# The small product on the identity, split in two and moved to the couple's end

## The chip, the cores and the metric

The kernel runs on one core of a Trainium2 chip, as one program. The metric is the device time of one execution in microseconds (us). A kernel's time is the median of its runs. TensorE multiplies matrices, VectorE and ScalarE work on elements and empty TensorE's results, GpSimd takes some element-wise work, and SyncE issues most transfers. In the profile they are PE (and PEld for its weight loads), DVE, ACT, POOL and SP.

## The reference

Attention with normalised queries and keys, and then a feed-forward block with SiLU. All is float32: 8 batches, 12 heads, 448 positions, head size 64; 768 model columns, 2048 inner columns.

```python
def rmsnorm(x, g):
    rms = np.sqrt(np.mean(x * x, axis=-1, keepdims=True) + 1e-06)
    return x / rms * g
q_n, k_n = (rmsnorm(q, g_q), rmsnorm(k, g_k))
scores = scale * np.matmul(q_n, k_n.transpose(0, 1, 3, 2))
scores = scores - np.max(scores, axis=-1, keepdims=True)
attn = np.exp(scores)
attn = attn / (np.sum(attn, axis=-1, keepdims=True) + 1e-09)
out = np.matmul(attn, v).astype(np.float32)
...
h = x @ w_in
g = h * (1.0 / (1.0 + np.exp(-h)))
return (g @ w_out).astype(np.float32)
```

Between the two blocks the heads of a position are laid side by side: `x` has 3584 rows of 768 columns.

## The kernel before

Two branches are built, and the inputs at hand take `bounded`. It works on "couples": four heads of one batch, that is, two pairs of heads. There are 24 couples (`NC`), and `c` counts them. Six couples (`GROUP`) make two batches. The order of work on each engine is the order in which the program issues it; nothing is rearranged by a scheduler. Tiles with several buffers rotate, and semaphores are put in where a buffer or a value is passed on.

For each couple the program runs `visit(c)` and then `between(c)`.

`visit(c)` issues the scores of couple c, their exponentials, and the weighing of the values with them. It begins with `scores(c, 0, 0)` (L750). Each `scores` takes the next of the two buffers of the PSUM tile `sc`; a buffer is two banks of 128 partitions x 512. The four products of a `scores` are 64x64 tiles of TensorE, at the four places of its array, and run beside each other. Each row half of the array writes a bank of its own. The same holds for `weigh` (L787), which adds into the banks `av0` and `av1`. Between two steps of the weighing, `turn` has VectorE or ScalarE copy one column into a bank (L763), and the weighing behind it waits for that copy.

`between(c)` prepares couple c+1 and does a share of the feed-forward product of the two batches finished before. That product is cut, in the manner of Strassen and Winograd, into seven products for each pair of blocks (`Seven`, L961), with additions on VectorE (L910) and GpSimd (L982, L985). Each of the seven is three matrix products with 128x128 weights and 448 columns. They go into the PSUM tile `mm` (two buffers) or, in some turns, into `sc`. `fill(others, prompt)` deals them out: it takes steps from the running product until the share is done. After every third step it issues the next entry of `prompt`; what is left of `prompt` and `others` comes at the end. A product may be cut by the end of a `fill` and be continued in the next.

The softmax sums of a couple are four products with `ones` (L830, 32 output partitions each). For most couples from 10 on (`LAGGED`) these are issued at the end of `between`, into `mm`; for the others they are issued before the second `fill`. The reciprocals of the sums (L839) follow on VectorE.

The change concerns the normalisation of the queries of later couples. From couple `LATE` = 9 on, the queries lie in "quarters" of 32 partitions: the 64 numbers of a head's row are cut into two runs of 32, which lie on neighbouring quarters. ScalarE squares them (`square`), VectorE adds up each run of 32 (`sum_squares`, L705) into a tile of 128 partitions x 28, and the two partial sums of a row have to be added across partitions. `scale(c)` does that on TensorE, with the matrix `ident`. It is the identity at first. At couple 7, `pair_up` copies each 32x32 identity block to the neighbouring quarter, so that each of the two 64x64 blocks on the diagonal holds four 32x32 identities and the rest is zero. One product with `ident` (L716) then gives both quarters the full sum. VectorE takes it from an `sc` buffer and applies 1/64 and the small constant (L717), GpSimd raises it to the power -1/2 (L720), and, from couple 12 on, GpSimd multiplies the rows of the queries with it (L729). For couples 9 to 11 VectorE does this multiplication, during the next visit (`scale_rows` in `weights_in_visit`).

`scale(c + 2)` is called in `between(c)` for c from 7 to 21, fifteen times. It is the last entry of the `prompt` of the second `fill`: the entries are the first of the softmax reciprocals, then the squares, the transposition of the keys (`flip`), the remaining entries with `sum_squares`, and `scale`. After that `fill` come `finish()` and `sum_x` at the end of a group of six, the softmax sums of a lagged couple (`sum_up`), a small activation on ScalarE (L1669) that has the table for the exponentials loaded, and then the next `visit`.

Of the kernel before, what the change touches and what calls it, by code (L numbers as in the profile page):

```python
# [542 lines left out]
def bounded(  # L543
# [3 lines left out]
    P, D, R, J, S = z.P, z.D, z.R, z.J, z.S  # L547
# [9 lines left out]
    GROUP, LATE = z.NPAIR, z.LATE  # L557
# [49 lines left out]
    def q_of(c):  # L607
        return rows_q[c % 2 if c < GROUP + 2 else 0]
# [101 lines left out]
    def scale(c):  # L710

        if c >= NC:
            return
        f = norm.rms[c % 2][:, 0:n]
        t = ps.tile([P, 2, BANK], F32, name="sc", bufs=2)[:, 0, 0:n]
        nc.tensor.matmul(t, ident, f, start=True, stop=True)  # L716
        nc.vector.tensor_scalar(  # L717
            out=f, in0=t, scalar1=1.0 / D, scalar2=1e-6, op0=ALU.mult, op1=ALU.add
        )
        nc.gpsimd.tensor_tensor(out=f, in0=f, in1=minus_half.to_broadcast([P, n]), op=ALU.pow)  # L720
        if c > SOON:
            scale_rows(c, nc.gpsimd)

    def scale_rows(c, engine):

        f = norm.rms[c % 2][:, 0:n]
        rows = q_of(c)[:, 0 : z.NK].rearrange("p (n e) -> p n e", e=z.Q)
        factor = f.rearrange("p (n one) -> p n one", one=1).to_broadcast([P, n, z.Q])
        engine.tensor_tensor(out=rows, in0=rows, in1=factor, op=ALU.mult)  # L729
# [75 lines left out]
    def sum_up(c):  # L805

        n = D // 2  # L810
        early = c < GROUP
        if c < GROUP:
            t = bank(S)
        elif c in LAGGED:
            t = ps_mm.tile([P, BANK], F32, name="mm")[:, 0:S]
        else:
            t = ps.tile([P, 2, BANK], F32, name="sc", bufs=2)[:, 0, 0:S]
        terms = [(0, lambda: weights(c, 0))]
        if early:
            terms = [(0, lambda: weights(c, LEFT - 1))] + terms + [(1, None)]  # L820
        if c in FULL:
            terms.insert(0, (1, None))
        if c == GROUP - 1:
            terms.insert(1, (0, lambda: weights(c, 1)))
        for k, (which, w) in enumerate(terms):
            if early and k == len(terms) - 2:
                yield
            for h in range(2):
                for i in range(2):
                    nc.tensor.matmul(  # L830
                        t[ds(h * D + i * n, n), :],
                        ones[:, which + i if which else 0],
                        left_weights(c)[:, h] if which else w()[:, i, h],
                        start=(k == 0), stop=(k == len(terms) - 1),
                    )

        def invert(half):
            rows = ts(half, S // 2)
            nc.vector.reciprocal(out=factors(c)[0][:, rows], in_=t[:, rows])  # L839

        def spread():
            mine = [a.rearrange("(h i p) s -> i h p s", h=2, i=2) for a in factors(c)]
            queues = (nc.sync, nc.gpsimd if c == GROUP - 1 else nc.sync)
            if c >= EARLY:
                nc.vector.tensor_copy(factors(c)[1], factors(c)[0])
                for i in range(2):
                    for h in range(2):
                        queues[h].dma_start(mine[i][1 - i, h], mine[i][i, h])
                return
            for h in range(2):  # L850
                for i in range(2):
                    nc.sync.dma_start(mine[1][i, h], mine[0][1, h])
            for h in range(2):
                nc.sync.dma_start(mine[0][1, h], mine[0][0, h])

        yield [lambda: invert(0), lambda: (invert(1), spread())]
# [160 lines left out]
    summed = set()  # L1017
# [552 lines left out]
    def run_all(work):  # L1570
        for piece in work:
            piece()

    def between(c):

        def transposes_and_sums():
            if c in LAGGED:
                first = [lambda: divide(c - 1, None)] if c - 1 in LAGGED else [lambda: None]
                return first + [lambda: None, lambda: flip(c + 1, "k"), gain]
            summing = sum_up(c)  # L1580
            if c < GROUP - 1:
                transpose_k(c + 1)
            if c < GROUP:
                next(summing)
            if c == GROUP - 1:
                reciprocals = next(summing)
                divide(c - 1, None)
                sum_x([0, 1], 0)
                run_all(reciprocals)
                return  # L1590
            if GROUP <= c < LATE - 1:
                transpose_k(c + 1)
            reciprocals = next(summing)
            if LATE - 1 <= c < NC - 1:
                reciprocals += [lambda: flip(c + 1, "k"), gain]
            if GROUP // 2 < c < EARLY:
                divide(c - 1, None)
            return reciprocals

        if c == GROUP - 1:  # L1600
            for _ in range(2):
                room.w_in.open()
            for i, t in enumerate(scratch):
                size = z.R, 2 * J * D
                rows = q_of(c + 2)[0 : z.R, ts(i, size[1])]
                nc.scalar.activation(t[0 : size[0], 0 : size[1]], rows, AF.Square)
            transposes_and_sums()
        if c < LATE - 1:
            transpose_q(c + 1)
        elif c < NC - 1:  # L1610
            flip(c + 1, "q")
        if c < GROUP // 2:
            inverting.extend(transposes_and_sums())
        elif c == GROUP - 1:
            transpose_k(c + 1)
        if c >= GROUP and c % GROUP == 0:
            fetched = range(AHEAD) if c == GROUP else ()
            columns = products - 2 * HW * S * len(fetched)
            work = halves_in(last_two(c), range(HF), plain_in, dict(begun), fetched, c + GROUP < NC)
            begin(work, columns, 2 * GROUP)  # L1620
            begun.clear()
        late = add(c, LEFT - 1) if c >= GROUP else []
        if c >= GROUP and c not in FULL:
            late += add(c, LEFT)
        further = normalise(c + 2) if c >= GROUP - 1 else []
        late += weights_in(c, 0)
        if c == GROUP:
            third, fourth = (
                [lambda i=i, step=step: sum_x(last_two(c), i, (step,)) for i in range(1, HW)]
                for step in (2, 3)  # L1630
            )
            late = third + late + fourth
        late += further[2:] if c >= GROUP else further[:2]
        if c - 1 in LAGGED and c not in LAGGED:
            late.append(lambda: divide(c - 1, None))
        if LATE - 1 <= c < SOON:
            late.insert(len(late) // 2, lambda: load_q(c + 2))
        fill(late)
        if LATE - 1 <= c < SOON:
            turns.update(least=8)  # L1640
        prompt = transposes_and_sums() if GROUP // 2 <= c != GROUP - 1 else []
        if prompt and c < GROUP:
            prompt.insert(0, lambda: None)
        if c == GROUP // 2:
            begin(make_ahead([0, 1]), AHEAD * 2 * HW * S, AHEAD * 2)
        if c >= LATE - 2:
            if c == LATE - 2:
                pair_up()
            squared = prompt[1:2] + [lambda: square(c + 2)]
            summed = prompt[3:] + [lambda: sum_squares(c + 2)]  # L1650
            steps = weights_in(c, 1)
            fill(
                steps + [lambda: None] * len(steps),
                prompt[0:1] + [lambda: run_all(squared)] + prompt[2:3]
                + [lambda: run_all(summed), lambda: scale(c + 2)],
            )
        else:
            fill(weights_in(c, 1) + (further[:2] if c >= GROUP else []), prompt)
        if c % GROUP == GROUP - 1:
            finish()  # L1660
            if c == GROUP - 1:
                begun[0] = fetch_ahead([0, 1], 0)
            elif c < NC - 1:
                sum_x([c // GROUP * 2, c // GROUP * 2 + 1], 0, range(2))
        if c in LAGGED:
            lagging.extend(next(sum_up(c)))
        if GROUP <= c < NC - 1:

            nc.scalar.activation(first, minus_half, AF.Exp)  # L1669
        if c == NC - 1:  # L1670
            while rounder.load():
                pass
# [28 lines left out]
    for m in range(2):  # L1701
        rows = [staged() for _ in range(2)]
# [215 lines left out]
```

## Time and profile before

| what | us |
| --- | --- |
| median of 3 runs | 1297.47 (1297.29 to 1297.59) |
| the profiled execution, its own time | 1297.48 |
| its span, first to last instruction | 1295.7 |
| TensorE busy | 1285.0, 99% of the span |
| VectorE busy | 966.5, 75% |
| the small product: 15 calls, 30 recorded passes | 0.189 to 0.273 each, median 0.268 |
| L705, sums of squares, VectorE, x15 | 1.076 each (median) |
| L717, VectorE, x15 | 0.187 each |
| L720, power on GpSimd, x15 | 4.795 each |
| L729, rows, on GpSimd x12, on VectorE x3 | 1.696 and 1.085 each |

The granted clock of TensorE was 0.998 over the whole span. A float32 product shows in the profile as two passes, each with its own weight load, so the counts of passes are twice those of products. The recorded length of a pass is modelled, and passes overlap: the distance between starts tells what a pass costs, not its length. The small products lie between 175 and 640 us of the span. After about 712 us the attention is over, and the second half of the feed-forward block runs alone (L1283).

### The profile page before, as it was taken

How to read it: one execution, taken by the hardware profiler on the slowest of the kernel's cores; microseconds unless marked ns; L12 is line 12 of the kernel's file. 1: busy time of each engine (PE TensorE's matmuls, PEld its weight loads, DVE VectorE, ACT ScalarE, POOL GpSimd, SP SyncE). 2: the span in 40 equal slices, each digit the busy share in tenths (PEclk: the TensorE clock that was granted, in tenths of full speed). 3: DMA queues.
4: the chain of work that ended last, by engine and by line, in shares of the span. 5: the costliest groups of instructions: out<-in, count | busy, mean ns of one | idle time of the engine just before them, and what ended most of it. 6: DMA issues, size and time to landing. Idle time of an engine off the chain costs nothing.

```text
span 1295.7 us, 19860 instructions
## 1 busy us (share of the span) xinstructions
PE 1285.0 (99%) x7182; PEld 831.5 (64%) x7182; DVE 966.5 (75%) x1672; ACT 503.9 (39%) x880; POOL 360.6 (28%) x221
## 2 busy tenths in 40 slices
PE   8999999999999999999999999999999999999998
PEld 4444444444444444444444555559999999999997
DVE  6899778768556558666555887798978787878785
ACT  7977566645555554554543344310001000000000
POOL 6756454533344344344311344400000000000000
PEclk9999999999999999999999999999999999999999
DMA  9674447434444444444411466312332313141411
GB/s 246 168 203 117 111 126 192 94 84 99 111 92 91 118 91 101 108 93 93 107 51 67 148 203 221 118 64 93 96 94 86 114 65 123 57 134 47 146 34 40
DMA packets 266160, 144.15 MB, mean 111 GB/s; under 512 B 203748, under 2 KB 249956, under 8 KB 266052
## 3 DMA queue, kind: packets, MB, share of 16 engines
q1 hardware_dynamic: 265424, 141.68, 39.6%
q8 instruction: 59, 0.97, 0.3%
q0 software_dynamic: 320, 0.90, 0.2%
q14 instruction: 49, 0.40, 0.1%
q10 hardware_dynamic: 308, 0.20, 0.1%
HBM read 95.36 MB, written 41.29 MB: 105 GB/s over the span
## 4 chain that ended last, share of the span: by engine, by line
PE 95%; DVE 2%; ACT 1%; SPq 1%; DMA 1%; issue 0%; ACTq 0%; DVEq 0%
PE alone L1283 23%; PE mm L961 19%; PE sc L961 11%; PE av L787 10%; PE sc L750 10%; PE mm L1283 8%; PE alone L961 7%; PE alone L1321 2%; PE mm L830 2%; PE mm L1321 1%; PE sc L643 1%; PE sc L674 0%; DMA rows<-in_k_dram 0%; PE sc L830 0%; DVE work L910 0%; SPq L255 0%
## 5 line engine op out<-in xcount | busy, mean ns | idle before, releaser
L755 ACT ACTIVATE work<-sc,rms 128x448 f32<-128x448 f32 x318 | 181.9, 635 | 97.2 <-PE sc L750 89.4
L750 PE MATMUL sc<-work 64*64 64x448 f32 x1344 | 164.8, 543 | 1.0 <-ACT work L653 0.6
L787 PE MATMUL av<-work,rows 64*64 64x448 f32 x1272 | 152.2, 540 | 0.3 <-DVE av L763 0.3
L961 PE MATMUL mm<-x,W 128*128 128x448 f32 x366 | 150.7, 544 | 0.0
L961 PE MATMUL mm<-sums_x,W 128*128 128x448 f32 x348 | 143.7, 544 | 0.0
L801 DVE TENSOR_TENSOR work<-work 128x896 f32<-128x896 f32 (+1 forms) x110 | 117.2, 1094 | 32.1 <-PE av L787 31.6
L530 POOL DMA_DIRECT2D out_dram<-x x2 | 1.2, 592 | 443.5 <-DVE x L910 443.5
L503 POOL TENSOR_TENSOR rms<-rms,minus_half 128x14 f32<-128x14 f32 (+4 forms) x40 | 97.4, 2437 | 86.9 <-DVE rms L499 82.2
L1283 PE MATMUL alone<-W,rows 128*128 128x192 f32 x610 | 113.0, 326 | 0.0
L961 PEld LDWEIGHTS mm<-x,W 128*128 128x128 f32 x366 | 67.8, 190 | 67.0 <-issue 61.8
L961 PEld LDWEIGHTS mm<-sums_x,W 128*128 128x128 f32 x348 | 64.7, 190 | 65.9 <-issue 60.5
L750 PEld LDWEIGHTS sc<-work 64*64 64x64 f32 x1344 | 54.7, 132 | 78.3 <-issue 29.7
L787 PEld LDWEIGHTS av<-work,rows 64*64 64x64 f32 x1272 | 59.9, 132 | 67.3 <-issue 32.6
L1283 PEld LDWEIGHTS alone<-W,rows 128*128 128x128 f32 x610 | 101.5, 190 | 0.0
L961 PE MATMUL sc<-x,W 128*128 128x448 f32 x246 | 99.6, 541 | 0.0
L982 POOL TENSOR_TENSOR stage<-parts,stage 128x448 f32<-128x448 f32 x31 | 39.1, 1262 | 174.5 <-ACT stage L981 174.1
L720 POOL TENSOR_TENSOR rms<-rms,minus_half 128x28 f32<-128x28 f32 x15 | 72.0, 4800 | 42.3 <-DVE rms L717 42.3
L961 PEld LDWEIGHTS sc<-x,W 128*128 128x128 f32 x246 | 46.4, 190 | 47.0 <-issue 46.9
L1283 PE MATMUL alone<-W,work 128*128 128x192 f32 x382 | 72.2, 326 | 0.0
L1293 ACT COPY rows<-alone 128x192 f32<-128x192 f32 x33 | 10.5, 317 | 141.6 <-PE alone L1283 141.6
L1114 ACT ACTIVATE stage<-stage 128x896 f32<-128x896 f32 x63 | 57.1, 945 | 17.6 <-DVE stage L910 17.2
L1283 PEld LDWEIGHTS alone<-W,work 128*128 128x128 f32 x382 | 63.8, 190 | 0.0
(267 smaller groups left out, 2307.0 us busy)
## 6 DMA issues: line engine op xcount, KB each, us to landing
hidden<-stage SPq DMA_DIRECT2D x63, 448.0 KB, 2.8
work<-hidden SPq DMA_DIRECT2D x21, 1024.0 KB, 5.1
rows<-in_moe_w_out_dram SPq DMA_DIRECT2D x32, 384.0 KB, 3.5
W<-in_moe_w_in_dram SPq DMA_DIRECT2D x22, 512.0 KB, 5.4
x<-hidden SPq DMA_DIRECT2D x7, 1024.0 KB, 5.5
rows<-in_q_dram SPq DMA_DIRECT2D x120, 56.0 KB, 2.2
rows<-in_k_dram SPq DMA_DIRECT2D x120, 56.0 KB, 2.2
rows<-in_k_dram SPq DMA_DIRECT2D x60, 96.0 KB, 2.6
```

Of the source, the lines that this page charges most:

```text
L503: nc.gpsimd.tensor_tensor(out=t, in0=t, in1=half, op=ALU.pow)
L720: nc.gpsimd.tensor_tensor(out=f, in0=f, in1=minus_half.to_broadcast([P, n]), op=ALU.pow)
L750: nc.tensor.matmul(two[ds(half * D, D), h, 0:S], keys[rows, ts(half, D)], qT[rows, pair, :], start=True, stop=True,)
L755: nc.scalar.activation(left_weights(c)[:, h] if j == LEFT else weights(c, j)[:, i, h], two[:, h, 0:S], AF.Exp, scale=norm.column(c, i, h, j),)
L787: nc.tensor.matmul(sums[i][ds(h * D, D), :], v, w, start=(j == 0 and step == 1), stop=(j == LEFT - 1 and step == 1),)
L801: nc.vector.tensor_tensor(out=total, in0=total, in1=more, op=ALU.add)
L830: nc.tensor.matmul(t[ds(h * D + i * n, n), :], ones[:, which + i if which else 0], left_weights(c)[:, h] if which else w()[:, i, h], start ...
L961: nc.tensor.matmul(t, self.left(name, s), self.right(name, s), start=s == ends[0], stop=s == ends[1])
L982: nc.gpsimd.tensor_tensor(out=done[1, 2], in0=u2, in1=p5, op=ALU.add)
L1114: nc.scalar.activation(t, t, AF.Silu)
L1283: nc.tensor.matmul(t, x[:, i], y, start=i == ORDER[0], stop=i == ORDER[-1])
L1321: nc.tensor.matmul(o, a[:, 2 * i + m, t], right_one(name, i)[:, m], start=n == 0, stop=n == len(steps) - 1,)
```

## The change

The product with `ident` becomes two, one for each 64x64 block on the diagonal: rows 0 to 63 of the array write partitions 0 to 63 of the result, rows 64 to 127 write partitions 64 to 127, in the same bank. The blocks left out hold zeros. The call of `scale(c + 2)` leaves the `prompt` of `fill` and comes after the softmax sums of a lagged couple, for the same couples 7 to 21. With the product move its three followers, L717 on VectorE, L720 and L729 on GpSimd.

```diff
@@ -713,7 +713,9 @@
             return
         f = norm.rms[c % 2][:, 0:n]
         t = ps.tile([P, 2, BANK], F32, name="sc", bufs=2)[:, 0, 0:n]
-        nc.tensor.matmul(t, ident, f, start=True, stop=True)
+        for h in range(2):
+            rows = ds(h * D, D)
+            nc.tensor.matmul(t[rows], ident[rows, rows], f[rows], start=True, stop=True)
         nc.vector.tensor_scalar(
             out=f, in0=t, scalar1=1.0 / D, scalar2=1e-6, op0=ALU.mult, op1=ALU.add
         )
@@ -1652,7 +1654,7 @@
             fill(
                 steps + [lambda: None] * len(steps),
                 prompt[0:1] + [lambda: run_all(squared)] + prompt[2:3]
-                + [lambda: run_all(summed), lambda: scale(c + 2)],
+                + [lambda: run_all(summed)],
             )
         else:
             fill(weights_in(c, 1) + (further[:2] if c >= GROUP else []), prompt)
@@ -1664,6 +1666,8 @@
                 sum_x([c // GROUP * 2, c // GROUP * 2 + 1], 0, range(2))
         if c in LAGGED:
             lagging.extend(next(sum_up(c)))
+        if c >= LATE - 2:
+            scale(c + 2)
         if GROUP <= c < NC - 1:

             nc.scalar.activation(first, minus_half, AF.Exp)
```

On TensorE the small product moves later by one matrix product (couples 8 to 11), two (12 to 21) or four (7), and in the lagged couples past the softmax sums too. On VectorE, L717 moves behind the addition of the last product that ends in the couple, and at couples 11 and 17 also behind two subtractions for the next group (`sum_x`, L907); at couples 9, 13, 16 and 19 its order stays. On GpSimd, L720 and L729 move behind one addition (L982 or L985) at couples 10, 13, 16 and 19; elsewhere the order stays.

## The prediction

> **What bounds the kernel now.** I read the page first: engine shares, then the chain that ended last.
>
> ```profile
> span 1295.7 us, 19860 instructions
> PE 1285.0 (99%) x7182; PEld 831.5 (64%) x7182; DVE 966.5 (75%) x1672; ACT 503.9 (39%) x880; POOL 360.6 (28%) x221
> PE 95%; DVE 2%; ACT 1%; SPq 1%; DMA 1%; issue 0%; ACTq 0%; DVEq 0%
> ```
>
> TensorE sets the end: it is busy 99% of the span and 95% of the chain. So a microsecond of TensorE time saved anywhere should be a microsecond of span, unless a wait takes its place. Next, the list of TensorE's own waits from 170 us (just before the first of the fifteen small products) to the end:
>
> ```profile
> PE sc L716 <- DVE rms L705: 0.6, 2, 0.4
> PE av L787 <- DVE av L763: 0.3, 1, 0.3
> ```
>
> Columns: microseconds in all, times, longest. Nothing else holds TensorE up, so nothing fixed in time (a transfer, another engine) stands behind it to eat a gain. And the one wait of note is at L716, the line of the change. Then the timeline of TensorE around two of the small products (start, length, group), the first at the end of couple 7, the other of couple 12:
>
> ```profile
> 170.60 2.42 PE L961 MATMUL sc<-x,W 128*128 128x448 f32 x6
> 172.86 2.42 PE L961 MATMUL mm<-x,W 128*128 128x448 f32 x6
> 175.53 0.38 PE L716 MATMUL sc<-rms,ident 128*128 128x28 f32 x2 [0.25 <-DVE rms L705]
> 175.74 2.50 PE L961 MATMUL mm<-sums_x,W 128*128 128x448 f32 x6
> 178.08 0.92 PE L961 MATMUL mm<-x,W 128*128 128x448 f32 x2
> 178.93 0.98 PE L750 MATMUL sc<-work 64*64 64x448 f32 x8
> ...
> 337.73 1.67 PE L961 MATMUL mm<-x,W 128*128 128x448 f32 x4
> 339.24 0.30 PE L716 MATMUL sc<-rms,ident 128*128 128x28 f32 x2
> 339.38 1.00 PE L961 MATMUL mm<-x,W 128*128 128x448 f32 x2
> 340.21 0.92 PE L961 MATMUL mm<-sums_x,W 128*128 128x448 f32 x2
> 341.15 0.96 PE L830 MATMUL mm<-work,ones 128*32 128x448 f32 x8
> 342.04 0.98 PE L750 MATMUL sc<-work 64*64 64x448 f32 x8
> ```
>
> A product is recorded as two passes. Six passes from 170.60 to 172.86 give the pitch: 0.376 us a pass of 448 columns. What a small product costs TensorE is then a subtraction. Couple 12: from 337.73 to 340.21 is 2.48 us, six long passes need 2.26, so the small one takes 0.22. Couple 7: 172.86 to 178.08 is 5.22, twelve passes need 4.51: 0.71. The recorded length of an L716 pass (0.19 to 0.27) is not what it costs. The weight loads explain the 0.22:
>
> ```profile
> 175.50 0.30 PEld L716 LDWEIGHTS sc<-rms,ident 128*128 128x128 f32 x2 [0.94 <-POOL stage L982]
> 178.93 0.21 PEld L750 LDWEIGHTS sc<-work 64*64 64x64 f32 x8 [0.65 <-issue]
> ```
>
> Each load of 128 columns is 0.186 to 0.190 us long, and two of them take 0.30, so the second starts 0.11 after the first. Beside a 0.376 pass such a load is hidden; beside 28 columns it isn't. Two loads are laid bare, that of the second pass and that of the product behind: 2 x 0.11 = 0.22.
>
> **The change part by part.**
>
> *The old place, removed.* The subtraction at all fifteen couples, 7 to 21, from the same timeline: 0.71, 0.81, 0.30, 0.22, 0.44, 0.22, 0.22, 0.22, 0.25, 0.22, 0.32, 0.22, 0.22, 0.22, 0.22. Sum 4.84 us. Of this 15 x 0.22 = 3.35 is the bare price, and 1.49 is lateness: the sums of squares (L705, 1.08 us on VectorE) are only just ready, at couples 7 and 8 above all (0.4 and 0.5 us). 4.84 us is also all the change can give.
>
> *The new place, added.* Two 64x64 products of two passes each, between the last full product (or the ones products of L830) and the scores (L750). TensorE changes its tile shape there already: 178.08 plus two passes is 178.83, the scores begin at 178.93, so 0.10 is paid today. The small product takes this and adds its own passes. No row shows 28 columns in a 64x64 tile, so I bound it. Below: 0, if everything fits in the shape change or beside the scores' other two tiles. Above: 0.54, two passes of the longest recorded length (0.27), if nothing overlaps. The nearest row is the 64x64 load: eight of them, each 0.13, start within 0.21 - 0.13 = 0.08 us; four go to four tiles some 7 ns apart, so the second round follows the first by 0.055 to 0.06, half of the 0.11 of 128 columns, as half the columns should. The two halves lie in different tiles and load together as the scores' four do. Laid bare are again two loads, of the second pass and of the scores: 2 x 0.055 = 0.11. That is the value I take. 15 x 0.11 = 1.65 us. If the halves went one after the other, four loads: 0.22, or 3.3 us.
>
> A rule of the Trainium skill speaks against this: "TensorEngine Tiling (Array Packing)", section Performance Considerations, gives each matmul some 60 cycles of overhead and advises against splitting what is already small. The trace's 28-column pass with its weights there has the next one starting 0.03 us later, so such a floor lies under the 0.055 of the load; by the rule alone the split brings nothing, and the sum would be the 3.3 us. The same page's Gotcha 1 says that different row tiles can't access one PSUM bank at the same time, and here both halves write one bank. No row shows two row tiles in one bank, and by the rule the halves would queue up: 3.3 us again.
>
> *Waits at the new place.* The sums of squares are ready one to four products earlier (0.75 us each), so the 1.49 goes. One small loss: at couple 10 the ones products take the bank that VectorE empties at 274.01 to 274.62; they would come 0.22 sooner and the emptying only a little: I set 0.06 us.
>
> *VectorE (L717, 0.19 us) moves*, in eleven couples behind the last product's addition (0.62 us). It ends some 0.6 us after the small product starts (175.53 to 175.94 + 0.19). Behind it in the lagged couples wait the reciprocal (L839) and the dummy copy (L763) that TensorE's next weighing needs; VectorE is idle 0.86 us before that copy at couple 12, which hides the 0.4 by which the reciprocal is later. The scores after next reuse the small product's buffer and wait for L717. At couple 17 the first scores start at 509.15 and these at 511.45, 2.3 us later, so some 1.8 us is spare. It is tight only at couples 11 and 17, where two subtractions go ahead of L717:
>
> ```profile
> 307.84 0.19 DVE L717 TENSOR_SCALAR rms<-sc 128x28 f32<-128x28 f32 x1
> 308.84 0.63 DVE L910 TENSOR_TENSOR stage<-mm,parts 128x448 f32<-128x448 f32 x1 [0.82 <-PE mm L961]
> 309.38 0.61 DVE L907 TENSOR_TENSOR sums_x<-x 128x448 f32<-128x448 f32 x1
> 310.03 0.62 DVE L907 TENSOR_TENSOR sums_x<-x,sums_x 128x448 f32<-128x448 f32 x1
> ```
>
> L717 would end near 310.8, 2.2 after the first scores (308.57): 0.1 to 0.2 spare. With the cover gone it costs about 0.1, twice. I count 0.
>
> *GpSimd (L720, 4.8 us, and L729, 1.7 us) moves* 1 to 3 us later, at couples 10, 13, 16 and 19 past one addition on its queue (L982 or L985), which thereby comes sooner. At couple 12 the queue then stands until 355.5 with L729 done at 346.4. At couples 7 to 9 what is behind is a rounding step of the weights (L137), about 1 us later, and VectorE's L729, which starts 3.1, 2.0 and 2.6 us after the power ends; the tightest, couple 8, keeps some 0.6. I count 0; without that cover VectorE is late by what is missing, against idle time like the 0.86 us at couple 12. No transfer moves.
>
> *Sum*, against the profiled execution's own time, 1297.48 (span 1295.7, and 1.78 around it; the median of the runs is 1297.47): 1297.48 - 4.84 + 1.65 + 0.06 = 1294.35.
>
> **The rivals.** *The halves queue up, or lateness stays.* For it: nothing shows two row tiles writing one bank. Against: four loads and four passes of the scores do start within 0.02 us. 1297.48 - 4.84 + 3.3 + 0.06 = 1296.0. If only the waits of couples 7 and 8 come back in another form, 1294.35 + 0.9 = 1295.3.
>
> *Nearly free.* The scores' two other tiles don't touch the small product's and could start beside it: for it, the loads' independence; against, they share TensorE's order. Cost 0 to 0.05 each: 1292.6 to 1293.4.
>
> *Slower: nothing overlaps at the shape change.* Scores behind a small product in the same two tiles have to let it run out, and each of the fifteen pays its recorded length, 2 x 0.27 = 0.54, or 8.1 us: 1297.48 - 4.84 + 8.1 = 1300.7. It decides from 0.32 us apiece (15 x 0.32 = 4.84). For it: the small product is now where no long pass hides its end. Against: at 175.74 a product followed 0.11 after a pass recorded as 0.27 long.
>
> **How the numbers follow.** The forecast has 0.66, the queued halves or left waits 0.20, nearly free 0.09, slower 0.05. Predicted 1294.3. Its own range is 1293.6 to 1295.0; for 8 in 10 I reach to the queued halves and halfway to the free case: 1293.0 to 1296.2. About 0.2% (2.6 us, so below 1294.9) can be told from no change. The forecast lies only 0.6 beyond that line, so I give four fifths of it and all of the free case to faster, and a little of the rest: 0.63. Slower has its 0.05; within 0.2% is left with 0.32.
>
> **What would show it.** After the change: the list of TensorE's waits without L705; the first scores 0.2 us (shape change and 0.11) behind the last product or ones pass, at all fifteen; the weight loads of the small product four in under 0.2 us; L717 done before the second scores. Wrong would be: 0.3 us or more between last pass and scores, halves 0.1 apart, or scores waiting for L717.

## The result, and the profile after

The changed kernel takes 1294.45 us (median of 14 runs), against 1297.61 for the kernel before in the same comparison. The ratio is 0.9976, with a 95% interval of 0.9967 to 0.9984: faster by 2.1 to 4.3 us. Beside other kernels it took 1294.32 (8 runs) against 1297.70, ratio 0.9973 (0.9962 to 0.9983). The executions of either kernel lie on two levels some 2 us apart, and the profile after is from the upper one (1296.34 us, span 1294.6), the one before from the lower.

The page of the profile after, the span and the chain that ended last:

```profile
span 1294.6 us, 19931 instructions
PE 97%; DVE 1%; POOL 1%; issue 0%; ACT 0%; DMA 0%; SPq 0%; ACTq 0%; DVEq 0%; POOLq 0%
```

TensorE still sets the end. Its own waits from 170 us on, which before were the wait for L705 and one more, are now one line:

```profile
PE av L789 <- DVE av L765: 0.3, 1, 0.3
```

The wait of the small product for the sums of squares is gone. In the new file the small product is L718, its VectorE step L719, the power L722, the products of the seven L963, the ones products L832, the scores L752, the weighing L789. TensorE's timeline at the end of couple 7, and then at couple 12:

```profile
175.06 2.42 PE L963 MATMUL mm<-x,W 128*128 128x448 f32 x6
177.32 2.42 PE L963 MATMUL mm<-sums_x,W 128*128 128x448 f32 x6
179.57 0.92 PE L963 MATMUL mm<-x,W 128*128 128x448 f32 x2
180.42 0.24 PE L718 MATMUL sc<-rms,ident 64*64 64x28 f32 x2
180.44 0.59 PE L752 MATMUL sc<-work 64*64 64x448 f32 x2
180.50 0.22 PE L718 MATMUL sc<-rms,ident 64*64 64x28 f32 x2
180.55 0.95 PE L752 MATMUL sc<-work 64*64 64x448 f32 x6
...
341.17 0.96 PE L832 MATMUL mm<-work,ones 128*32 128x448 f32 x8
342.06 0.24 PE L718 MATMUL sc<-rms,ident 64*64 64x28 f32 x2
342.08 0.59 PE L752 MATMUL sc<-work 64*64 64x448 f32 x2
342.13 0.22 PE L718 MATMUL sc<-rms,ident 64*64 64x28 f32 x2
342.19 0.95 PE L752 MATMUL sc<-work 64*64 64x448 f32 x6
```

Eight long passes from 177.32 end at 180.33 by the pitch of 0.376, and the small product starts 0.09 later: the shape change, and no wait. From 175.06 to 179.57 the long passes follow one another with nothing between (4.51 us, twelve passes). Both halves start at 180.42 (7 ns apart in the records). Then the trace shows something finer than was expected: two passes of the scores start at 180.44, ahead of the small product's second passes at 180.50. They are in the two tiles that the small product leaves free. The other two tiles begin the scores some 0.14 after the small product's start (the group at 180.55). So the scores don't all start 0.2 us behind the last long product, as the prediction had put down: two of the four tiles start 0.11 behind it and two 0.23.

The whole gain can be read off two pairs of lines. The product pass of couple 7 that started at 172.86 before starts at 175.06 after, 2.20 us later: that lies ahead of the change. The last group of TensorE's passes, before and then after:

```profile
1287.89 1.46 PE L1283 MATMUL alone<-W,work 128*128 128x192 f32 x8
```

```profile
1286.97 1.46 PE L1285 MATMUL alone<-W,work 128*128 128x192 f32 x8
```

So the stretch from couple 7 to the end went from 1287.89 - 172.86 = 1115.03 to 1286.97 - 175.06 = 1111.91: 3.12 us shorter. From couple 22 on the two traces run with the same distance to 0.01 us; nothing is given back.

### The profile page after: what moved, and what is told of

Same layout as the page of the kernel before. It is cut to its first block, busy times and chain, and to the rows that moved or that the text cites. A ratio compares the mean times of both kernels' runs of the same rounds, so it can differ in the third digit from the quotient of the medians.

```text
span 1294.6 us, 19931 instructions
## 1 busy us (share of the span) xinstructions
PE 1283.5 (99%) x7212; PEld 840.7 (65%) x7212; DVE 971.4 (75%) x1672; ACT 504.3 (39%) x880; POOL 363.5 (28%) x221
## 4 chain that ended last, share of the span: by engine, by line
PE 97%; DVE 1%; POOL 1%; issue 0%; ACT 0%; DMA 0%; SPq 0%; ACTq 0%; DVEq 0%; POOLq 0%
PE alone L1285 23%; PE mm L963 21%; PE sc L963 11%; PE av L789 10%; PE sc L752 10%; PE mm L1285 8%; PE alone L963 7%; PE alone L1323 2%; PE mm L832 2%; PE mm L1323 1%; PE sc L643 1%; PE sc L832 1%; PE sc L674 0%; DVE work L912 0%; POOL rms L503 0%
## 5 line engine op out<-in xcount | busy, mean ns | idle before, releaser
L752 PE MATMUL sc<-work 64*64 64x448 f32 x1344 | 169.4, 543 | 1.0 <-ACT work L653 0.6
L789 PE MATMUL av<-work,rows 64*64 64x448 f32 x1272 | 155.5, 540 | 1.2 <-DVE x L1514 0.9
L963 PE MATMUL mm<-x,W 128*128 128x448 f32 x366 | 149.1, 542 | 0.0
L963 PE MATMUL mm<-sums_x,W 128*128 128x448 f32 x348 | 142.4, 542 | 0.0
L963 PEld LDWEIGHTS mm<-x,W 128*128 128x128 f32 x366 | 68.5, 190 | 70.3 <-issue 64.8
L963 PEld LDWEIGHTS mm<-sums_x,W 128*128 128x128 f32 x348 | 65.1, 190 | 68.1 <-issue 62.5
L789 PEld LDWEIGHTS av<-work,rows 64*64 64x64 f32 x1272 | 65.9, 132 | 62.8 <-issue 19.3
L752 PEld LDWEIGHTS sc<-work 64*64 64x64 f32 x1344 | 60.4, 132 | 63.3 <-ACT work L757 25.3
L963 PE MATMUL sc<-x,W 128*128 128x448 f32 x246 | 99.6, 541 | 0.0
L722 POOL TENSOR_TENSOR rms<-rms,minus_half 128x28 f32<-128x28 f32 x15 | 72.6, 4842 | 48.9 <-DVE rms L719 47.8
L963 PEld LDWEIGHTS sc<-x,W 128*128 128x128 f32 x246 | 46.4, 190 | 47.0 <-issue 46.7
```

Source lines behind the costliest of these rows:

```text
L752: nc.tensor.matmul(two[ds(half * D, D), h, 0:S], keys[rows, ts(half, D)], qT[rows, pair, :], start=True, stop=True,)
L789: nc.tensor.matmul(sums[i][ds(h * D, D), :], v, w, start=(j == 0 and step == 1), stop=(j == LEFT - 1 and step == 1),)
L963: nc.tensor.matmul(t, self.left(name, s), self.right(name, s), start=s == ends[0], stop=s == ends[1])
```

## The experiments

Single times differ by more than these edits, so the instrument was the trace: the starts of TensorE's passes, without the small product's, set one by one against those of the kernel before, from the last products ahead of couple 7's small product to the end. The difference, taken from the 4.84 us that the small product cost before, is what it costs in each kernel:

| kernel | small product | from couple 7 to the end, against before, us | cost of the small product, us | median, us |
| --- | --- | --- | --- | --- |
| before | whole, old place | 0 | 4.84 | 1297.41 to 1297.70 |
| split_old | split, old place | +2.26 | 7.10 | 1299.89 |
| whole_new | whole, behind the sums | -0.76 | 4.08 | 1297.02 |
| split_before_sums | split, ahead of the sums | -2.42 | 2.42 | 1294.82 |
| whole_before_sums | whole, ahead of the sums | -3.13 | 1.71 | 1294.58 |
| after, and again | split, behind the sums | -3.12, -3.12 | 1.72 | 1294.45, 1294.32 |
| doubled | split, twice, behind the sums | -1.46 | 3.38 | 1296.16 |
| two_banks | split, into two banks | -2.95 | 1.89 | 1294.76 (one run) |
| no_product | none | -4.79 | 0.05 | 1292.66 |
| mixed | split, whole in four couples | -3.46 | 1.38 | 1294.27 |

**The split alone.**

```diff
-        nc.tensor.matmul(t, ident, f, start=True, stop=True)
+        for h in range(2):
+            rows = ds(h * D, D)
+            nc.tensor.matmul(t[rows], ident[rows, rows], f[rows], start=True, stop=True)
```

> The split alone, at the old place among the 128x128 products. Theory (shape changes and bare weight loads): each small product now has a shape change before it (0.09 us gap), two bare loads of 64 columns (2 x 0.055), and a change back to 128x128 (0.09, and 0.10 for the first load of 128 columns, which lies bare), about 0.4 us in place of 0.22; with the lateness of 1.5 us left as it is, 15 x 0.18 = 2.7 us slower than before, near 1300.2. Rival (the split itself is the gain, half the columns to load): 15 x 0.11 = 1.7 us faster than before, near 1295.8.

Measured: 2.26 us slower from couple 7 on; in the whole time 1299.89 against 1297.41, ratio 1.0020 (1.0010 to 1.0029). Couple 12 in its timeline:

```profile
340.18 1.67 PE L963 MATMUL mm<-x,W 128*128 128x448 f32 x4
341.78 0.30 PE L718 MATMUL sc<-rms,ident 64*64 64x28 f32 x4
342.01 1.02 PE L963 MATMUL mm<-x,W 128*128 128x448 f32 x2
342.87 0.92 PE L963 MATMUL mm<-sums_x,W 128*128 128x448 f32 x2
```

Four passes from 340.18 end at 341.68, the small product comes 0.10 later. From 340.18 to 342.87 are 2.69 us, six long passes need 2.26: it costs 0.43, where the whole product cost 0.22. The two shape changes, 0.09 us each, take more than the loads of half the columns save. At couples 7, 8, 9 and 11, all of them with lateness, the loss is only 0.03 to 0.06: there the shape change seems to fall into the wait, and so it is 2.26 in all and not 2.7. The rival, that the split is the gain, is out.

**The move alone, and the place ahead of the softmax sums.** whole_new undoes the split in the changed kernel. split_before_sums keeps the split and puts the call ahead of the sums, and whole_before_sums has the whole product there. This is the edit of the place, against the changed kernel:

```diff
-        if c in LAGGED:
-            lagging.extend(next(sum_up(c)))
         if c >= LATE - 2:
             scale(c + 2)
+        if c in LAGGED:
+            lagging.extend(next(sum_up(c)))
```

> The move alone: one 128x128 product behind the softmax sums. Theory: in the five couples without lagged sums the weights are loaded ahead and only the second load (0.11 us) lies bare; in the ten with them there is a shape change from the ones products (0.09) and two bare loads of 128 columns (0.22), 0.31 in all. Sum 5 x 0.11 + 10 x 0.31 = 3.7 us against 4.84 before and 1.7 after: 1.2 us faster than before, 2 us slower than the changed kernel. Rival (the place is worth nothing beyond the lateness): 15 x 0.22 = 3.3 us.

> The changed kernel with the small product ahead of the lagged softmax sums instead of behind them. Theory: nothing changes in the five couples without lagged sums (0.11 us each); in the ten others there is one more shape change, 128x128 to 64x64 to 128x32, so 0.09 + 0.11 = 0.20 each: 2.6 us in all, 0.9 slower than the changed kernel. Where the ones products wait for their bank anyway (0.09 us in four couples) up to 0.09 of it is hidden. Rival (a shape change is free, being overlapped): no difference from the changed kernel.

> No split: one 128x128 product, after the last product of the couple and ahead of the lagged softmax sums. Theory: its first weights are loaded beside the long pass ahead of it, only the second load (0.11 us) lies bare, and the load behind it is laid bare by the shape change anyway: 15 x 0.11 = 1.7 us, as the changed kernel, 3.1 us faster than before; up to 0.09 us in each of four couples is hidden behind the wait of the ones products, so perhaps 0.3 better than the changed kernel. Rival (the split halves the loads): 15 x 0.22 = 3.3 us, 1.6 slower than the changed kernel.

Measured: -0.76, -2.42 and -3.13 us; ratios to the kernel before 0.9995 (0.9986 to 1.0005), 0.9979 (0.9969 to 0.9989) and 0.9974 (0.9963 to 0.9985). Each is nearer to the theory's number (-1.2, -2.2, -3.1) than to its rival's, but the first misses by 0.44. The whole product behind the ones products, with a shape change of its own, costs 0.34 in a lagged couple, where 0.31 was expected, and 0.14 in the five without lagged sums, where 0.11 was expected: some 0.03 short in all fifteen. The third is the instructive one. Couple 13 of whole_before_sums:

```profile
371.95 1.67 PE L961 MATMUL mm<-x,W 128*128 128x448 f32 x4
373.45 0.30 PE L716 MATMUL sc<-rms,ident 128*128 128x28 f32 x2
373.68 0.96 PE L830 MATMUL mm<-work,ones 128*32 128x448 f32 x8
```

Four passes end at 373.45 and the small product starts there, its weights loaded ahead; the ones products follow 0.23 later, of which 0.09 is the shape change that is there anyway. So 0.14 is left, against 0.22 in the middle of the products: the bare load of the second pass, 0.11, and the 0.03 between the starts of the two passes, which the theory had left out. That the total is as expected is partly luck. Eleven couples cost about 0.14 instead of 0.11, and the four in which the ones products wait for their bank only 0.05, since the wait covers the rest. In all, a whole product at the end of a run of the same shape is worth as much here as the split at the beginning of the next (1.71 against 1.72).

**What the product still costs.** The product is left out, so the sums over two quarters are not formed; VectorE reads the partial sums. The buffer goes with it, and no scores have to wait for VectorE's step.

```diff
-        t = ps.tile([P, 2, BANK], F32, name="sc", bufs=2)[:, 0, 0:n]
-        for h in range(2):
-            rows = ds(h * D, D)
-            nc.tensor.matmul(t[rows], ident[rows, rows], f[rows], start=True, stop=True)
         nc.vector.tensor_scalar(
-            out=f, in0=t, scalar1=1.0 / D, scalar2=1e-6, op0=ALU.mult, op1=ALU.add
+            out=f, in0=f, scalar1=1.0 / D, scalar2=1e-6, op0=ALU.mult, op1=ALU.add
         )
```

> The changed kernel without the small product: VectorE takes the partial sums of squares as they are, so the sum over the two neighbouring quarters is left out. It shows what the product still costs at the new place. Theory: 15 x 0.11 = 1.7 us faster than the changed kernel, 4.8 faster than before. Rival (nearly free at the new place): no more than 0.5 us faster than the changed kernel; rival (something behind it waits for VectorE's step): over 3 us faster.

Measured: -4.79 us, ratio 0.9958 (0.9941 to 0.9974). That is 1.67 less than the changed kernel, and all but 0.05 of the 4.84 that the subtraction in the timeline of before had given. So the ceiling was read rightly, and the product isn't nearly free at its new place.

**What sets the price at the new place.** The halves are issued twice over:

```diff
-        for h in range(2):
+        for h in (0, 1, 0, 1):
```

> The changed kernel with the two halves issued twice over, in the same two tiles. Theory (each further pass in a tile lays bare one load of 64 columns): 2 x 0.055 us more in each of fifteen couples, 1.65 us slower than the changed kernel. Rival (a fixed cost of the shape change, passes free): no change. Rival (each matmul instruction has its own cost, tiles or not): twice the product's cost, 1.7 us at the four passes more, but then with the halves' starts 0.05 apart instead of a few ns.

Measured: 3.12 - 1.46 = 1.66 us slower than the changed kernel, 0.11 for two more passes in each tile; ratio to before 0.9987 (0.9978 to 0.9997). Couple 12 in the timeline:

```profile
339.97 0.96 PE L832 MATMUL mm<-work,ones 128*32 128x448 f32 x8
341.11 0.95 PE L752 MATMUL sc<-work 64*64 64x448 f32 x6
```

From the ones products to the scores in the small product's tiles are 1.14 us; in the changed kernel they are 1.02 (341.17 to 342.19). The price goes by passes in the same tile, 0.055 each, and the two halves, in different tiles and starting 7 ns apart, don't add up. Nor is it a price of the pass as such: with the same 28 columns, a further pass takes 0.11 us behind 128 weight columns and 0.055 behind 64, and in this trace the weight loads of one tile follow one another by 0.055 to 0.059. That passes are free and only the shape change costs is out. So is the slower rival of the prediction: passes that had to run out, at the 0.22 us of their recorded length, would have cost four times this.

**One bank or two.**

```diff
-        t = ps.tile([P, 2, BANK], F32, name="sc", bufs=2)[:, 0, 0:n]
+        t = ps.tile([P, 2, BANK], F32, name="sc", bufs=2)[:, :, 0:n]
...
-            nc.tensor.matmul(t[rows], ident[rows, rows], f[rows], start=True, stop=True)
+            nc.tensor.matmul(t[rows, h], ident[rows, rows], f[rows], start=True, stop=True)
```

(VectorE's step is made once for each half.)

> The changed kernel with the second half in the other bank of its buffer, and VectorE's step in two of 64 partitions. Theory (two row tiles may write one bank at once): the starts of the small product's passes and of the scores behind it as in the changed kernel, to 0.01 us. Rival (row tiles queue for a bank): the passes and scores come 0.05 us or more sooner in each couple.

Measured, in a single execution and by its trace: the small product's passes and the scores behind them start as in the changed kernel to 0.001 us. So one bank was no hindrance. The 0.17 us by which it is slower lies in couples 11 and 17 alone, 0.085 each, and shows another step of the prediction. The loads of the scores that reuse the buffer, in the lists of waits of the changed kernel and of two_banks:

```profile
PEld sc L752 <- DVE rms L719: 0.9, 2, 0.4
```

```profile
PEld sc L755 <- DVE rms L721: 1.3, 2, 0.6
```

In both the loads wait for VectorE's step, twice, but in the changed kernel TensorE itself doesn't lose by it. One more VectorE instruction of about 0.18 us ahead, and TensorE loses 0.085: the cover in these two couples is about 0.1 us.

**A mixture.** Per couple, the whole product ahead of the sums was cheaper than the split behind them where the ones products wait for their bank, at couples 12, 15, 18 and 21.

```diff
+        ahead_of_sums = c in LAGGED and c % 3 == 0
+        if c >= LATE - 2 and ahead_of_sums:
+            scale(c + 2, True)
         if c in LAGGED:
             lagging.extend(next(sum_up(c)))
-        if c >= LATE - 2:
+        if c >= LATE - 2 and not ahead_of_sums:
             scale(c + 2)
```

> The changed kernel, but in couples 12, 15, 18 and 21 one 128x128 product ahead of the softmax sums, where the ones products wait for their bank anyway. The small product cost there 0.05 us in the kernel with whole products ahead of the sums, against 0.10 to 0.14 in the changed kernel. Theory (costs are set couple by couple and add up): 0.26 us faster than the changed kernel from couple 7 to the end, 3.4 us faster than the kernel before. Rival (the gain of one couple is taken back by the next, where a wait is waiting): no difference from the changed kernel. In the whole time 0.26 us is 0.02% and can't be told.

Measured: -3.46 us, 0.34 better than the changed kernel by the trace, where 0.26 was expected. From couple 12 on, where the edit lies, it is 0.28; the rest, 0.08 at couple 11 less 0.02 at couple 7, lies ahead of the edit and stays unexplained. So the costs of the couples add up, to a few hundredths. In the whole time 1294.27 against 1297.58, ratio 0.9974 (0.9964 to 0.9984), which can't be told from the changed kernel.

## Why the prediction was right

*What bounds the kernel.* That a saving on TensorE reaches the end undiminished was right: 3.12 us were gained by couple 22, and 3.12 at the end.

*The old place removed, 4.84 us.* Right: without any product 4.79 came free. The part called lateness did go with the move: at couples 7 and 8 the distance shrank by 0.59 and 0.69, as 0.71 and 0.81 less the new price. (The lateness of these two is 0.49 and 0.59 by the prediction's own subtraction, where its text says 0.4 and 0.5; the sum has the right values.)

*The new place, 15 x 0.11 = 1.65.* Measured 1.72, or 0.114 each. The reason given, two bare loads of 64 columns in tiles that work side by side, stands: doubling added 0.055 for each pass and tile. Two rules of the Trainium skill, "TensorEngine Tiling (Array Packing)", were set against it. Gotcha 1 there has row tiles unable to use one bank at once. In these runs no queue shows: the halves, on different partitions, start 7 ns apart in one bank, and two banks change nothing. The page's advice against splitting what is small fits the old place (0.43 in place of 0.22), where the shape changes cost, and not the place behind the softmax sums (0.11 in place of 0.34).

*The loss of 0.06 at couple 10* wasn't there: the couple gained 0.135 where 0.22 less 0.114 is 0.11. What the prediction missed is that VectorE's step for the small product left the place ahead of the addition that empties the bank. So the emptying came as much sooner as the ones products: they start 0.136 us after the long pass ahead of them has ended in the kernel before, and 0.129 in the kernel after.

*The moved steps.* VectorE's was counted at 0, with a cover of 0.1 to 0.2 us at couples 11 and 17. Couple 11 of the profile after, VectorE and then TensorE:

```profile
310.68 0.18 DVE L719 TENSOR_SCALAR rms<-sc 128x28 f32<-128x28 f32 x1
```

```profile
310.99 1.01 PE L752 MATMUL sc<-work 64*64 64x448 f32 x8
```

L719 ends at 310.86, 0.13 ahead of the scores that need it. The prediction named scores waiting for this step as a sign of being wrong, and it half came: the loads of these scores waited, twice, but their passes started on time. GpSimd's power and rows, later by some microseconds, stand in no wait of TensorE.

*The sum.* -4.84 + 1.65 + 0.06 = -3.13, measured -3.12; 1294.35 worked out, 1294.45 measured. The closeness of the last two is partly luck, since single executions differ by up to 2.5 us.

*The rivals.* Queued halves: out, by the starts and by the two banks. Nearly free: its mechanism is real, since the scores' free tiles do start beside the small product, but the price measured, 0.114, is that of the other two, whose scores start 0.14 after it; so it earned little. Slower by passes running out: out, by the doubled product.

What the prediction didn't see is that the split was not needed for the gain. Of the five new combinations of form and place in the table it costed one; the whole product ahead of the sums does the same, helped by the wait in four couples.

## What to carry to other kernels

The tiny matrix product of this kernel was paid in weight loads laid bare and in shape changes, and hardly in its columns: read such a price from the distance between the long passes around it. Put it where a shape change or a bare load is paid anyway, and keep its shape that of a neighbour; a split into smaller tiles in the middle of full-size products cost more than it saved here. Move it late enough that its input isn't just being made, and then look for the next user of its buffer.

## What the runs showed of the hardware

Passes don't start in the order in which the products were issued when they are in different tiles: the scores' passes at 180.44 started between the two passes of the small product issued before them, at 180.42 and 180.50. Had the passes started in the order of issue, those at 180.44 would have come behind the one at 180.50.

A shape change shows as 0.093 us between the end of a pass (by the pitch) and the next start, for each change in the traces before and after, from 170 us on, that waited for nothing else: 128x128 to 64x64 and to 128x32, and 128x32 to 64x64 and to 128x128; from 64x64 back to 128x128 it is 0.090. Behind it the first load lies bare: the distance to the second pass is 0.48 us into 128 columns, 0.43 into 64 and 0.40 into 32, instead of 0.376.

The stretch ahead of couple 7, where all eleven profiled kernels are alike, differs between them by up to 2.3 us. In the profile after, one of the longest, the chain that ended last runs there through GpSimd (start, length, piece; "issue" is time with no cause in the profile):

```profile
75.11 1.30 POOL W L137
76.41 2.24 issue
78.65 0.04 POOLq L518
78.69 1.64 POOL rms L503
```

In the kernel before the chain stays on TensorE from 70 to 90 us. What brings GpSimd into the chain in some executions was not tried and stays open.
